# A recurrent attention and mixer kernel: own-step products from PSUM, a new order of work, two units turned by DMA, deeper buffers

## The chip, the cores and the metric

The kernel runs on one core of a Trainium2 chip. A core has five engines with a queue of instructions each: TensorE (PE) multiplies matrices out of SBUF into PSUM, VectorE (DVE) and ScalarE (ACT) work element by element on both memories, GpSimd (POOL) does so on SBUF alone, and SyncE (SP) issues DMA transfers. POOL issues transfers too. The metric is the device time of one execution in microseconds; smaller is better.

## The reference

Four batches, eight heads, 768 steps, 48 columns per head. A state of 48 x 48 per head decays by w in each step and takes in the outer product of k and v. The output of a step reads the state before it, and the step's own product with a weight u in place of the state. The result goes through a mixer: two matrices over the steps (768 to 256 to 768), then two over the columns (384 to 1536 to 384), each pair with a ReLU between and a residual sum.

```python
for t in range(S):
    cur = einsum('bhd,bhe->bhde', u * k[t], v[t])
    y[t] = einsum('bhd,bhde->bhe', r[t], state + cur)
    state = w * state + einsum('bhd,bhe->bhde', k[t], v[t])
h = maximum(xt @ w_tok1, 0) @ w_tok2
u = x + h^T
out = u + maximum(u @ w_ch1, 0) @ w_ch2
```

## The kernel before

A unit is 128 steps of one batch with all eight heads; a batch has six units, numbered 0 to 23 through the batches. Three units make a group, after which the state is carried on (`G = 3`).

The order of all work is written out by hand as a string, `PLAN`. Each word is a step: a letter for the kind, and a unit or indices. The steps are traced in this order, and every engine keeps the order in which its own instructions were traced, so a step that waits holds up all that its engine has behind it. A capital letter is the same step on another engine, mostly DVE. The letters:

- `l0`, `l1`, `l2`: the next load of k, r or v, 192 KB, issued on SP. The n-th load of each belongs to unit n. The list `FIRST` issues k0, k1, r0 and k2 ahead of the plan. `AFTER` makes the load of k with a given number wait until a part of the weights has landed; since SP works in order, all later loads wait behind it. There are seven buffers for each of k, r and v.
- `D`: one of six tables of decay (`wkr`), written by ACT. `C`: small constants.
- `k`, `r` (POOL) or `K`, `R` (DVE): k or r of a unit times its decay, into a tile `kr` with both. `NK` such tiles are used in turn.
- `a`: PE turns the eight blocks of `kr` into one PSUM bank (`kr_ps`, k's half and r's half), and ACT copies the whole to `krT`. `q`: the same with the copy split, k's half by ACT and r's half by DVE. `A`: a DMA transpose issued by SP in place of both.
- `o`: own product, `krT`'s k half times its r half on DVE. `e` / `E`: four small matmuls of it on PE and a copy to `adg` by ACT / DVE. `y` / `Y`: `yd` = v times `adg`, on POOL / DVE.
- `v` / `V`: v as bfloat16 (`vb`) by ACT / DVE. `b`: the scores (`at_ps`) on PE, masked by DVE into `AT`. `s` / `S`: the unit's k and v into the state sum (`kv_ps`) on PE, copied by ACT / DVE (twice 48 partitions), or, for the last unit of a group, scaled by DVE. `c`: the unit's output `y_ps` on PE, plus `yd` on DVE into `x_b`.
- `h`, `g`: the mixer over the steps; `n` / `N` / `t`: the turned `uT` by PE with a copy by ACT / DVE, or by a DMA transpose. `u` / `U`: 128 of the 1536 hidden columns, three matmuls into `z_ps` and a ReLU into `zr` by ACT / DVE. `d`: six matmuls into `h_ps` (h2), after the second half a sum by DVE and a store issued by SP.
- `W`: a part of the weights, issued by POOL in its own order, numbered 0 to 6: 0 and 1 the step matrices, 2 to 4 the up matrix in pieces of 3, 3 and 6 blocks, 5 and 6 the halves of the down matrix.
- `x`: one dummy matmul that keeps PE busy.

PSUM has one bank or two for the scores, the state sum and the output, with one buffer of each (`psA`), and a pool of four banks for all the rest, the dummy matmuls too (`psM`, tag `m`). A bank is free again when all its readers are done.

Engine instructions carry the line of a helper (L68) in the profile, so groups go by tile names.

Of the kernel before, what the change touches and what calls it, by code (L numbers as in the profile page):

```python
# [22 lines left out]
def kernel(  # L23
# [373 lines left out]
    PLAN = """
    l1 D0.0 l1 D0.1 K1 K0 D1.0 l2 D0.2 D1.2 R0 K2 l0 D1.1 x r1 a0 v0 C0 l2 o0 r2 C1 a1 l1 r3 b0
    K3 l1 l0 a2 x e0 x y0 l2 o1 l2 o2 s0 x x x x x x x e1 a3 C2 v1 e2 b1 l0 r4 c0 l1 l2 x x x x
    x x b2 l2 x v2 y1 S1 k4 o3 K5 q4 x x x x x e3 y2 W0 c1 o4 v3 b3 r5 l2 a5 o5 l1 c2 s2 l0 l0  # L400
    W1 x W2 x l1 v5 x x e4 l2 y4 b4 y3 c3 e5 V4 s3 h0.0 b5 y5 W4 x x x s4 c4 h0.1 x c5 h0.2 h0.3
    h0.4 W3 h0.5 g0.1 g0.0 g0.2 l1 g0.5 n0.1 N0.2 N0.0 g0.4 N0.5 k6 l0 l2 g0.3 U0.0.2 u0.0.0
    n0.3 l0 U0.0.7 n0.4 r6 l2 U0.0.8 q6 l1 u0.1.7 u0.0.11 K7 u0.0.6 v6 u0.1.9 o6 r7 U0.0.1
    u0.1.0 W5 R8 l0 u0.0.3 q7 l1 u0.0.9 u0.1.3 u0.0.10 l2 K8 l1 u0.0.5 U0.1.11 u0.1.2 u0.1.6 V7
    e6 U0.1.5 a8 b6 o7 S6 u0.1.4 Y6 U0.0.4 l0 o8 u0.1.1 u0.1.10 e7 W6 y7 l2 b7 d0.1.0 r10 s7 K9
    d0.0.0 k10 l0 c6 E8 b8 R9 l1 u0.1.8 v10 l2 l1 d0.0.1 V9 l1 l0 l2 c7 R11 d0.1.1 a9 l0 d0.2.0
    o9 y8 v8 d0.3.0 S8 c8 b9 a10 e9 l1 K11 d0.2.1 s9 y9 c9 b10 o10 a11 d0.3.1 d0.4.0 k12 o11 r13
    e10 r12 d0.4.1 l0 Y10 c10 v11 v12 l2 l0 e11 b11 s10 Y11 h1.0 d0.5.0 l1 l1 a12 h1.1 c11 v13
    o12 h1.2 h1.3 k13 l0 h1.4 R14 l2 h1.5 l0 d0.5.1 r15 l0 l0 l2 E12 l2 g1.2 g1.0 g1.1 l1 g1.4
    n1.0 k14 n1.2 b12 n1.1 n1.4 g1.5 a13 g1.3 u1.0.0 u1.0.7 o13 l1 Y12 U1.0.1 n1.3 E13 Y13 k15  # L410
    s12 l1 u1.0.4 b13 n1.5 a14 u1.0.5 c12 a15 l2 k16 u1.0.6 o14 U1.0.2 l0 o15 u1.0.3 c13 s13
    u1.0.10 R17 E14 l2 e15 b14 r16 u1.0.8 a16 k17 v14 U1.1.2 l1 u1.0.11 Y14 V15 l0 b15 d1.0.0
    S14 u1.0.9 a17 l2 b16 c14 k18 v16 V17 Y15 d1.1.0 d1.0.1 o16 c15 d1.1.1 U1.1.5 s15 o17 b17
    e16 r19 U1.1.1 r18 y16 l0 c16 E17 l2 v18 s16 l1 u1.1.0 l1 y17 u1.1.3 a18 V20 u1.1.4 o18 k19
    u1.1.6 u1.1.7 c17 h2.0 A19 R20 k21 v19 d1.2.0 E18 b18 l2 k20 R21 h2.1 Y18 h2.2 d1.2.1 h2.3
    o19 h2.4 h2.5 s18 b19 a20 c18 E19 u1.1.8 u1.1.10 o20 v21 r22 l2 g2.0 t2.0 y19 g2.2 c19 g2.5
    e20 a21 g2.1 g2.4 k22 y20 s19 b20 t2.2 o21 u1.1.9 t2.4 r23 n2.1 U1.1.11 g2.3 V23 k23 s20 A22
    c20 u2.0.0 V22 t2.3 b21 E21 u2.0.2 d1.3.0 u2.0.8 d1.3.1 U2.0.6 U2.0.4 b22 o22 n2.5 Y21
    u2.0.1 u2.0.5 U2.0.3 d1.4.0 d1.5.0 u2.1.3 A23 b23 e22 o23 d1.4.1 S21 d1.5.1 e23 u2.0.11 c21
    u2.1.5 Y22 u2.0.7 U2.0.10 Y23 u2.0.9 d2.0.0 c22 u2.1.2 S22 h3.0 h3.1 d2.0.1 c23 h3.2 d2.1.0  # L420
    h3.3 h3.4 u2.1.9 h3.5 d2.1.1 g3.0 g3.1 t3.1 g3.2 d2.2.0 t3.2 t3.0 d2.2.1 u2.1.1 u2.1.7
    u2.1.6 u2.1.4 u2.1.10 g3.3 t3.3 g3.4 U2.1.8 U2.1.0 g3.5 u3.0.1 u3.0.10 U3.0.5 U3.0.6 U2.1.11
    d2.4.0 u3.0.8 t3.4 u3.0.2 t3.5 d2.3.0 d2.4.1 U3.1.1 U3.1.4 U3.1.7 d2.3.1 u3.1.8 U3.0.9
    u3.0.11 U3.1.5 u3.0.3 u3.1.6 U3.0.4 u3.1.0 u3.1.2 U3.1.3 d2.5.0 U3.0.0 d2.5.1 u3.1.11 u3.0.7
    d3.0.0 u3.1.9 u3.1.10 d3.0.1 d3.2.0 d3.2.1 d3.1.0 d3.1.1 d3.5.0 d3.5.1 d3.3.0 d3.4.0 d3.3.1
    d3.4.1
    """
# [31 lines left out]
```

## Time and profile before

| | us |
|---|---|
| median of 3 runs | 174.02 (173.68 to 175.73) |
| the profiled execution, its own time | 173.81 |
| its span | 172.1 |
| granted clock of PE | full throughout |
| ACT busy in the span | 78.6 |
| POOL busy in the span | 50.5 |
| DMA queue of SP | 20.65 MB, 57.8% of the 16 engines' span |
| DMA queue of POOL | 3.15 MB, 11.8% |

The profile shows one execution. A group's row has the line, the engine, the operation, out<-in with tile names, shapes and the number of instructions; behind the bar stand the busy time, the mean of one in ns, and the idle time of the engine before them with what ended it. A timeline's row has the start, the time to the end of the last of the merged instructions, and in brackets the idle time before it. A row of a DMA issue ends with the time from issue to landing. Matmuls overlap, so the duration of a merged matmul row holds more than its share of the engine: eight transposes take 0.45 us when others follow. Weight loads of PE (PEld) run beside matmuls.

### The profile page before, as it was taken

How to read it: one execution, taken by the hardware profiler on the slowest of the kernel's cores; microseconds unless marked ns; L12 is line 12 of the kernel's file. 1: busy time of each engine (PE TensorE's matmuls, PEld its weight loads, DVE VectorE, ACT ScalarE, POOL GpSimd, SP SyncE). 2: the span in 40 equal slices, each digit the busy share in tenths (PEclk: the TensorE clock that was granted, in tenths of full speed). 3: DMA queues.
4: the chain of work that ended last, by engine and by line, in shares of the span. 5: the costliest groups of instructions: out<-in, count | busy, mean ns of one | idle time of the engine just before them, and what ended most of it. 6: DMA issues, size and time to landing. Idle time of an engine off the chain costs nothing.

```text
span 172.1 us, 3977 instructions
## 1 busy us (share of the span) xinstructions
PE 163.1 (95%) x1570; PEld 103.8 (60%) x1570; DVE 121.6 (71%) x231; ACT 78.6 (46%) x172; POOL 50.5 (29%) x61
## 2 busy tenths in 40 slices
PE   6999789899999999999999999899999999999992
PEld 3555565566666766567667677556665655656560
DVE  5476996974797999999997899885655272631312
ACT  3895342179635355399627476331412522334000
POOL 2159946260017392533244919000000000000000
PEclk9999999999999999999999999999999999999999
DMA  5999899999989998999968962540211241201222
GB/s 111 225 221 223 133 196 209 199 150 173 200 176 179 216 236 235 216 230 195 217 141 188 126 140 50 107 107 6 91 41 50 57 107 23 91 0 50 91 91 91
DMA packets 89532, 24.05 MB, mean 140 GB/s; under 512 B 82729, under 2 KB 89514, under 8 KB 89514
## 3 DMA queue, kind: packets, MB, share of 16 engines
q1 hardware_dynamic: 85664, 20.65, 57.8%
q0 software_dynamic: 3824, 3.15, 11.8%
q8 instruction: 12, 0.20, 0.5%
q14 instruction: 6, 0.05, 0.1%
q10 hardware_dynamic: 26, 0.00, 0.0%
HBM read 20.45 MB, written 4.72 MB: 146 GB/s over the span
## 4 chain that ended last, share of the span: by engine, by line
PE 68%; DVE 13%; DMA 6%; issue 5%; ACT 3%; POOL 2%; SPq 1%; POOLq 0%
PE z_ps L68 24%; PE h_ps L68 23%; PE kr_ps L68 4%; PE idle_ps L68 3%; DMA uT<-u_sb 3%; PE y_ps L68 3%; PE at_ps L68 3%; DVE AT L68 2%; DVE x_b L68 2%; PE hT_ps L68 2%; DMA rt<-in_r_dram 2%; DVE own L68 2%; ACT wkr L68 2%; PE kv_ps L68 2%; PE t_ps L68 2%
## 5 line engine op out<-in xcount | busy, mean ns | idle before, releaser
L68 PE MATMUL z_ps<-uT,wch 128*128 128x384 bf16 x288 | 53.6, 326 | 0.8 <-DMA uT<-u_sb 0.8
L68 PE MATMUL h_ps<-wch,zr 128*128 128x384 bf16 x288 | 52.2, 326 | 0.1
L68 ACT ACTIVATE zr<-z_ps 128x384 bf16<-128x384 f32 x66 | 31.7, 494 | 37.6 <-PE z_ps L68 37.4
L68 PEld LDWEIGHTS <-zr 128*128 128x128 bf16 x288 | 27.2, 98 | 17.6 <-DVE zr L68 0.5
L68 PEld LDWEIGHTS <-wch 128*128 128x128 bf16 x288 | 26.6, 98 | 16.7 <-DMA uT<-u_sb 0.6
L68 DVE TENSOR_TENSOR AT<-at_ps,mask 128x1024 bf16<-128x1024 f32 x24 | 29.2, 1215 | 4.1 <-PE at_ps L68 4.1
L68 DVE TENSOR_TENSOR osb<-u_sb,h_ps 128x384 f32<-128x384 bf16 x24 | 13.2, 550 | 18.2 <-PE h_ps L68 18.2
L68 ACT COPY krT<-kr_ps 128x1024 bf16<-128x1024 bf16 (+1 forms) x21 | 20.0, 952 | 8.4 <-PE kr_ps L68 7.8
L68 POOL TENSOR_TENSOR kr<-rt,wkr 128x384 bf16<-128x384 f32 x16 | 17.0, 1071 | 18.5 <-DMA rt<-in_r_dram 9.3
L68 DVE TENSOR_SCALAR zr<-z_ps 128x384 bf16<-128x384 f32 x30 | 16.2, 554 | 8.2 <-PE z_ps L68 8.0
L68 POOL TENSOR_TENSOR kr<-kt,wkr 128x384 bf16<-128x384 f32 x15 | 15.9, 1069 | 12.3 <-PE kv_ps L68 7.0
L68 PEld LDWEIGHTS <-kr 128*128 128x128 bf16 x248 | 16.6, 102 | 4.6 <-issue 0.7
L68 POOL TENSOR_TENSOR yd<-vt,adg 128x384 f32<-128x384 f32 x13 | 11.5, 885 | 25.1 <-DVE yd L68 10.5
L68 DVE TENSOR_TENSOR own<-krT 128x512 bf16<-128x512 bf16 x24 | 13.5, 568 | 3.0 <-ACT krT L68 2.9
L68 DVE TENSOR_TENSOR x_b<-y_ps,yd 128x384 bf16<-128x384 f32 x24 | 13.2, 549 | 2.4 <-PE y_ps L68 1.9
L68 PEld LDWEIGHTS <-krT 48*128 48x128 bf16 (+1 forms) x272 | 10.6, 96 | 6.4 <-issue 3.1
L68 PE MATMUL idle_ps<-warm 128*128 128x512 bf16 x38 | 13.1, 465 | 1.4 <-DVE warm L68 1.4
L68 PE MATMUL kr_ps<-ident,kr 128*128 128x128 bf16 x168 | 14.1, 232 | 0.1
L68 DVE TENSOR_TENSOR u_sb<-x_b,hT_ps 128x384 bf16<-128x384 bf16 x24 | 12.1, 544 | 2.6 <-PE hT_ps L68 2.6
L68 PEld LDWEIGHTS <-wtok 128*128 128x128 bf16 x96 | 8.3, 97 | 5.2 <-issue 1.0
L68 ACT CAST S<-kv_ps 48x192 bf16<-48x192 f32 x24 | 7.5, 313 | 7.7 <-PE kv_ps L68 5.8
L68 PE MATMUL hT_ps<-h1r,wtok 128*128 128x384 bf16 x48 | 10.2, 325 | 0.6 <-ACT h1r L68 0.4
(59 smaller groups left out, 141.5 us busy)
## 6 DMA issues: line engine op xcount, KB each, us to landing
kt<-in_k_dram SPq DMA_DIRECT2D x24, 192.0 KB, 3.8
rt<-in_r_dram SPq DMA_DIRECT2D x24, 192.0 KB, 3.8
vt<-in_v_dram SPq DMA_DIRECT2D x24, 192.0 KB, 3.8
out_dram<-osb SPq DMA_DIRECT2D x24, 192.0 KB, 1.9
wch<-in_moe_w_ch_dram POOLq DMA_DIRECT2D x3, 576.0 KB, 8.3
wtok<-in_moe_w_tok_dram POOLq DMA_DIRECT2D x2, 384.0 KB, 7.4
wch<-in_moe_w_ch_dram POOLq DMA_DIRECT2D x2, 288.0 KB, 9.6
uT<-u_sb SPq DMA_TRANSPOSE x10, 2.3
```

The costliest lines, as they stand in the source:

```text
L68: return lambda *args, **kw: tc.keep_in_program_order(f(*args, **kw))
```

## The change

- `AFTER`: the loads of k8 and k9 both wait for part 3 of the weights. Before, k9 alone waited, for part 2.
- `NK` from 4 to 6, and six buffers of `krT` in place of four.
- A new step `O`: own product with k's half read from `kr_ps` in PSUM and r's half from `krT` in SBUF. It is used for units 0, 1, 2, 3, 4, 6, 11, 12 and 15. The bank `kr_ps` is held until it has run.
- Units 20 and 21 are turned by a DMA transpose (`A`), not by PE and ACT.
- The order is new up to there, with some steps on another engine, among them: k0 on POOL and r1 on DVE; v1 by DVE, v4 by ACT; the copies of adg for units 1 and 3 by DVE; yd of 2 and 4 by DVE; the state copies of unit 1 by ACT; unit 5 with the split copy; r7 by DVE. 24 dummy matmuls stand in the plan in place of 30. From the mixer of batch two on, the order is as before.

```diff
-    AFTER = {9: 2}
+    AFTER = {9: 3, 8: 3}
...
-    NK = 4
+    NK = 6
...
     def turned(n, halves=False):
         L = live[n]
-        krT = apool.tile([128, 2, HP, T], bf16, name="krT")
+        krT = apool.tile([128, 2, HP, T], bf16, name="krT", bufs=6)
         L["kT"], L["rT"] = krT[:, 0], krT[:, 1]
-        kr_ps = psM.tile([128, 2, HP, T], bf16, name="kr_ps", tag="m")
+        kr_ps = L["kr_ps"] = psM.tile([128, 2, HP, T], bf16, name="kr_ps", tag="m")
...
     def turned_by_dma(n):
         L = live[n]
-        krT = apool.tile([128, 2, HP, T], bf16, name="krT")
+        krT = apool.tile([128, 2, HP, T], bf16, name="krT", bufs=6)
...
-    def own_product(n):
+    def own_product(n, from_psum=False):
         L = live[n]
         L["own"] = apool.tile([128, HP, T], bf16, name="own")
-        dve.tensor_mul(L["own"], L["kT"], L["rT"])
+        dve.tensor_mul(L["own"], L["kr_ps"][:, 0] if from_psum else L["kT"], L["rT"])
...
-        o=own_product, e=own_sum, E=lambda n: own_sum(n, copy), y=own_part, Y=lambda n: own_part(n, dve),
+        o=own_product, O=lambda n: own_product(n, True), e=own_sum, E=lambda n: own_sum(n, copy), y=own_part, Y=lambda n: own_part(n, dve),
...
     PLAN = """
-    l1 D0.0 l1 D0.1 K1 K0 D1.0 l2 D0.2 D1.2 R0 K2 l0 D1.1 x r1 a0 v0 C0 l2 o0 r2 C1 a1 l1 r3 b0
-    K3 l1 l0 a2 x e0 x y0 l2 o1 l2 o2 s0 x x x x x x x e1 a3 C2 v1 e2 b1 l0 r4 c0 l1 l2 x x x x
-    x x b2 l2 x v2 y1 S1 k4 o3 K5 q4 x x x x x e3 y2 W0 c1 o4 v3 b3 r5 l2 a5 o5 l1 c2 s2 l0 l0
-    W1 x W2 x l1 v5 x x e4 l2 y4 b4 y3 c3 e5 V4 s3 h0.0 b5 y5 W4 x x x s4 c4 h0.1 x c5 h0.2 h0.3
-    h0.4 W3 h0.5 g0.1 g0.0 g0.2 l1 g0.5 n0.1 N0.2 N0.0 g0.4 N0.5 k6 l0 l2 g0.3 U0.0.2 u0.0.0
-    n0.3 l0 U0.0.7 n0.4 r6 l2 U0.0.8 q6 l1 u0.1.7 u0.0.11 K7 u0.0.6 v6 u0.1.9 o6 r7 U0.0.1
-    u0.1.0 W5 R8 l0 u0.0.3 q7 l1 u0.0.9 u0.1.3 u0.0.10 l2 K8 l1 u0.0.5 U0.1.11 u0.1.2 u0.1.6 V7
-    e6 U0.1.5 a8 b6 o7 S6 u0.1.4 Y6 U0.0.4 l0 o8 u0.1.1 u0.1.10 e7 W6 y7 l2 b7 d0.1.0 r10 s7 K9
-    d0.0.0 k10 l0 c6 E8 b8 R9 l1 u0.1.8 v10 l2 l1 d0.0.1 V9 l1 l0 l2 c7 R11 d0.1.1 a9 l0 d0.2.0
...
-    u1.1.6 u1.1.7 c17 h2.0 A19 R20 k21 v19 d1.2.0 E18 b18 l2 k20 R21 h2.1 Y18 h2.2 d1.2.1 h2.3
-    o19 h2.4 h2.5 s18 b19 a20 c18 E19 u1.1.8 u1.1.10 o20 v21 r22 l2 g2.0 t2.0 y19 g2.2 c19 g2.5
-    e20 a21 g2.1 g2.4 k22 y20 s19 b20 t2.2 o21 u1.1.9 t2.4 r23 n2.1 U1.1.11 g2.3 V23 k23 s20 A22
...
+    l1 x l1 D0.0 D1.0 l1 D0.2 x l0 D1.2 x R0 D1.1 x k0 x D0.1 K2 K1 a0 l2 C0 v0 l1 R1 a1 C1 K3 x
+    r2 O0 b0 l2 O1 e0 l2 y0 r3 l0 x a2 s0 x x V1 b1 r4 l2 x x k4 O2 E1 x a3 O3 x e2 l0 C2 x s1 y1
+    l1 l2 l0 x b2 v2 l2 c0 l0 S2 W0 q4 K5 x l1 c1 W1 O4 x Y2 v3 l2 b3 E3 r5 x e4 q5 l2 l1 c2 x y3
+    v4 W2 s3 b4 o5 x x x Y4 c3 x h0.0 v5 x e5 s4 b5 h0.1 W4 c4 h0.2 y5 c5 h0.3 h0.4 l1 h0.5 g0.1
+    g0.0 W3 g0.2 g0.5 n0.1 N0.2 N0.0 g0.4 g0.3 n0.5 k6 U0.0.2 U0.0.7 l0 n0.4 u0.0.8 U0.0.0 r6 l2
+    l1 n0.3 K7 u0.0.11 u0.0.6 q6 u0.1.2 u0.1.7 l2 l0 l1 U0.1.9 W5 R7 v6 O6 l0 U0.0.1 b6 u0.1.3
+    u0.0.3 l2 u0.0.9 R8 U0.1.0 q7 K8 u0.0.5 u0.0.10 U0.1.11 l1 e6 V7 s6 u0.1.6 a8 u0.1.4 l0 s7 o7
+    U0.1.5 l1 U0.1.1 l2 E7 u0.1.10 W6 o8 Y6 U0.0.4 c6 b7 d0.1.0 Y7 e8 l0 d0.0.0 v9 d0.0.1 l1 l0
...
+    e9 l1 K11 d0.2.1 y9 c9 s9 l0 b10 o10 a11 d0.3.1 l2 d0.4.0 E10 R13 v11 k12 O11 d0.4.1 Y10 v12
+    c10 r12 e11 s10 l0 h1.0 b11 Y11 h1.1 l0 d0.5.0 l2 l1 l0 a12 R14 c11 O12 r15 k13 l1 v13 l1
...
+    u1.0.5 l2 l2 k16 a14 c12 a15 l0 o14 u1.0.3 c13 s13 O15 U1.0.10 v14 E14 r17 l1 r16 b14 K17
...
+    l2 s16 l1 d1.0.1 l1 y17 u1.1.3 a18 V20 u1.1.4 R20 k21 o18 k19 u1.1.6 u1.1.7 c17 R21 h2.0 k20
+    A19 v19 d1.2.0 E18 b18 l2 h2.1 Y18 A20 h2.2 d1.2.1 h2.3 o19 h2.4 h2.5 s18 b19 c18 E19 u1.1.8
+    u1.1.10 o20 v21 r22 A21 l2 g2.0 t2.0 y19 g2.2 c19 g2.5 e20 g2.1 g2.4 k22 y20 s19 b20 t2.2 o21
...
```

More of the change, by code (lines that the diff above doesn't have):

```diff
@@ L404 @@
-    u0.1.0 W5 R8 l0 u0.0.3 q7 l1 u0.0.9 u0.1.3 u0.0.10 l2 K8 l1 u0.0.5 U0.1.11 u0.1.2 u0.1.6 V7
-    e6 U0.1.5 a8 b6 o7 S6 u0.1.4 Y6 U0.0.4 l0 o8 u0.1.1 u0.1.10 e7 W6 y7 l2 b7 d0.1.0 r10 s7 K9
-    d0.0.0 k10 l0 c6 E8 b8 R9 l1 u0.1.8 v10 l2 l1 d0.0.1 V9 l1 l0 l2 c7 R11 d0.1.1 a9 l0 d0.2.0
-    o9 y8 v8 d0.3.0 S8 c8 b9 a10 e9 l1 K11 d0.2.1 s9 y9 c9 b10 o10 a11 d0.3.1 d0.4.0 k12 o11 r13
-    e10 r12 d0.4.1 l0 Y10 c10 v11 v12 l2 l0 e11 b11 s10 Y11 h1.0 d0.5.0 l1 l1 a12 h1.1 c11 v13
-    o12 h1.2 h1.3 k13 l0 h1.4 R14 l2 h1.5 l0 d0.5.1 r15 l0 l0 l2 E12 l2 g1.2 g1.0 g1.1 l1 g1.4
@@ L410 @@
[L410 to L414, printed above, removed]
-    u1.1.6 u1.1.7 c17 h2.0 A19 R20 k21 v19 d1.2.0 E18 b18 l2 k20 R21 h2.1 Y18 h2.2 d1.2.1 h2.3
@@ L416 @@
-    o19 h2.4 h2.5 s18 b19 a20 c18 E19 u1.1.8 u1.1.10 o20 v21 r22 l2 g2.0 t2.0 y19 g2.2 c19 g2.5
-    e20 a21 g2.1 g2.4 k22 y20 s19 b20 t2.2 o21 u1.1.9 t2.4 r23 n2.1 U1.1.11 g2.3 V23 k23 s20 A22
[L418 to L426, printed above, removed]
+    l1 x l1 D0.0 D1.0 l1 D0.2 x l0 D1.2 x R0 D1.1 x k0 x D0.1 K2 K1 a0 l2 C0 v0 l1 R1 a1 C1 K3 x
+    r2 O0 b0 l2 O1 e0 l2 y0 r3 l0 x a2 s0 x x V1 b1 r4 l2 x x k4 O2 E1 x a3 O3 x e2 l0 C2 x s1 y1
@@ new lines @@
+    R10 u0.1.8 k10 R9 l2 v8 l2 d0.3.0 b8 d0.1.1 l1 v10 k9 l0 c7 R11 S8 a9 d0.2.0 o9 y8 c8 b9 a10
+    e9 l1 K11 d0.2.1 y9 c9 s9 l0 b10 o10 a11 d0.3.1 l2 d0.4.0 E10 R13 v11 k12 O11 d0.4.1 Y10 v12
+    c10 r12 e11 s10 l0 h1.0 b11 Y11 h1.1 l0 d0.5.0 l2 l1 l0 a12 R14 c11 O12 r15 k13 l1 v13 l1
+    h1.2 h1.3 h1.4 h1.5 d0.5.1 g1.2 g1.0 g1.1 l2 n1.2 l0 g1.4 n1.0 b12 l1 g1.3 l2 e12 n1.1 K14
+    a13 k15 n1.4 l0 U1.0.1 y12 u1.0.7 u1.0.0 o13 N1.3 g1.5 u1.0.2 E13 Y13 l1 u1.0.4 s12 b13 N1.5
+    u1.0.5 l2 l2 k16 a14 c12 a15 l0 o14 u1.0.3 c13 s13 O15 U1.0.10 v14 E14 r17 l1 r16 b14 K17
@@ new lines @@
+    u1.0.8 U1.0.11 u1.1.2 y14 e15 a16 V15 b15 l0 l2 d1.0.0 V17 U1.0.6 u1.0.9 S14 b16 a17 V16 k18
+    d1.1.0 Y15 c14 o16 U1.1.5 d1.1.1 c15 o17 s15 e16 u1.1.1 y16 l0 r18 b17 u1.1.0 r19 c16 e17 V18
+    l2 s16 l1 d1.0.1 l1 y17 u1.1.3 a18 V20 u1.1.4 R20 k21 o18 k19 u1.1.6 u1.1.7 c17 R21 h2.0 k20
+    A19 v19 d1.2.0 E18 b18 l2 h2.1 Y18 A20 h2.2 d1.2.1 h2.3 o19 h2.4 h2.5 s18 b19 c18 E19 u1.1.8
+    u1.1.10 o20 v21 r22 A21 l2 g2.0 t2.0 y19 g2.2 c19 g2.5 e20 g2.1 g2.4 k22 y20 s19 b20 t2.2 o21
+    u1.1.9 t2.4 r23 n2.1 U1.1.11 g2.3 V23 k23 s20 A22 c20 u2.0.0 V22 t2.3 b21 E21 u2.0.2 d1.3.0
@@ new lines @@
+    u2.0.8 d1.3.1 U2.0.6 U2.0.4 b22 o22 n2.5 Y21 u2.0.1 u2.0.5 U2.0.3 d1.4.0 d1.5.0 u2.1.3 A23
+    b23 e22 o23 d1.4.1 S21 d1.5.1 e23 u2.0.11 c21 u2.1.5 Y22 u2.0.7 U2.0.10 Y23 u2.0.9 d2.0.0 c22
+    u2.1.2 S22 h3.0 h3.1 d2.0.1 c23 h3.2 d2.1.0 h3.3 h3.4 u2.1.9 h3.5 d2.1.1 g3.0 g3.1 t3.1 g3.2
+    d2.2.0 t3.2 t3.0 d2.2.1 u2.1.1 u2.1.7 u2.1.6 u2.1.4 u2.1.10 g3.3 t3.3 g3.4 U2.1.8 U2.1.0 g3.5
+    u3.0.1 u3.0.10 U3.0.5 U3.0.6 U2.1.11 d2.4.0 u3.0.8 t3.4 u3.0.2 t3.5 d2.3.0 d2.4.1 U3.1.1
+    U3.1.4 U3.1.7 d2.3.1 u3.1.8 U3.0.9 u3.0.11 U3.1.5 u3.0.3 u3.1.6 U3.0.4 u3.1.0 u3.1.2 U3.1.3
@@ L427 @@
+    d2.5.0 U3.0.0 d2.5.1 u3.1.11 u3.0.7 d3.0.0 u3.1.9 u3.1.10 d3.0.1 d3.2.0 d3.2.1 d3.1.0 d3.1.1
+    d3.5.0 d3.5.1 d3.3.0 d3.4.0 d3.3.1 d3.4.1
     """
```

## The prediction

> **What bounds the kernel now.** I read the page first, then the windows of the stages, the groups by form, and the timelines of DVE, POOL and SP up to 50 us.
>
> ```profile
> span 172.1 us, 3977 instructions
> PE 163.1 (95%) x1570; PEld 103.8 (60%) x1570; DVE 121.6 (71%) x231; ACT 78.6 (46%) x172; POOL 50.5 (29%) x61
> ...
> 9.00:29.50 20.50, 18.54 (x237) 11.74 (x237) 17.52 (x27) 10.69 (x28) 13.93 (x17) 1.00 1.17 194
> ...
> 33.60:47.00 13.40, 13.40 (x115) 8.64 (x113) 8.83 (x19) 10.00 (x21) 2.65 (x3) 1.00 1.13 173
> 47.00:70.00 23.00, 22.68 (x274) 15.40 (x272) 21.17 (x37) 10.50 (x23) 11.62 (x11) 1.00 0.96 209
> 70.00:97.00 27.00, 26.83 (x332) 18.53 (x332) 24.94 (x46) 18.75 (x41) 11.64 (x13) 1.00 0.92 193
> 97.00:108.00 11.00, 10.62 (x138) 7.40 (x135) 10.74 (x21) 5.76 (x13) 6.37 (x7) 1.00 0.59 93
> ...
> 33.63 0.65 PE L68 MATMUL z_ps<-uT,wch 128*128 128x384 bf16 x3
> ```
>
> The window rows give the stretch, then busy time of PE, PEld, DVE, ACT and POOL, granted clock, DMA share and GB/s. From 33.6 us, where the first up-projection starts, PE works without gaps (13.40 of 13.40, 22.68 of 23, 26.83 of 27). Before that PE is filled with dummy matmuls, and DVE is the busiest of the others, 17.52 of 20.50 us. From 97 to 108 us DVE is full (10.74 of 11). So three things can move the end: when the first z starts; PE work after it; and stalls of PE in between. The window 33.6 to 97 holds only 0.5 us of PE idle, so almost nothing is to be gained there and much can be lost.
>
> **The start, to 33.6 us.** Units 0 to 5 pass through DVE in order.
>
> ```profile
> 9.00:29.50 20.50, 4.70 (x6) 1.00 1.17 194
> ...
> L68 DVE TENSOR_TENSOR own<-krT x24: 406/417/1236, 9.4 to 119.3; 128x512 bf16<-128x512 bf16 x24
> ...
> 11.93 1.00 POOL L68 TENSOR_TENSOR kr<-rt,wkr 128x384 bf16<-128x384 f32 x1 [2.12 <-DMA rt<-in_r_dram]
> 12.88 1.01 POOL L68 TENSOR_TENSOR yd<-vt,adg 128x384 f32<-128x384 f32 x1
> ...
> 11.96 2.20 DVE L68 TENSOR_TENSOR own<-krT 128x512 bf16<-128x512 bf16 x2
> 15.28 1.22 DVE L68 TENSOR_TENSOR AT<-at_ps,mask 128x1024 bf16<-128x1024 f32 x1 [1.11 <-PE at_ps L68]
> ...
> 17.32 1.22 DVE L68 TENSOR_TENSOR AT<-at_ps,mask 128x1024 bf16<-128x1024 f32 x1 [0.36 <-PE at_ps L68]
> ...
> 28.72 0.56 DVE L68 TENSOR_TENSOR x_b<-y_ps,yd 128x384 bf16<-128x384 f32 x1 [0.71 <-PE y_ps L68]
> ```
>
> The first row is DVE's own products alone: six take 4.70 us, where six of the median 417 ns take 2.50. The other 2.20 us are stretch: two own products from 11.96 to 14.16 us ran while POOL was at kr and yd (11.93 to 13.89). The masks (AT) and x_b, which read one operand from PSUM, keep 1.22 and 0.56 us beside POOL work, so own products with k's half in PSUM should lose the stretch. Their own duration isn't in the trace:
>
> ```profile
> L68 DVE TENSOR_TENSOR AT<-at_ps,mask 128x1024 bf16<-128x1024 f32 x24 | 29.2, 1215 | 4.1 <-PE at_ps L68 4.1
> ...
> L68 DVE TENSOR_TENSOR x_b<-y_ps,yd 128x384 bf16<-128x384 f32 x24 | 13.2, 549 | 2.4 <-PE y_ps L68 1.9 <-POOL yd L68 0.3
> ...
> L68 DVE TENSOR_TENSOR yd<-vt,adg 128x384 f32<-128x384 f32 x11 | 6.8, 614 | 0.1
> ...
> L68 DVE COPY adg<-ad_ps 128x8 f32<-128x8 f32 x8 | 1.2, 153 | 0.1
> ...
> L68 DVE COPY krT<-kr_ps 128x512 bf16<-128x512 bf16 x3 | 1.3, 424 | 1.6 <-ACT krT L68 1.5
> ...
> L68 DVE CAST S<-kv_ps 48x192 bf16<-48x192 f32 x8 | 2.8, 352 | 0.2
> ```
>
> Between 549 ns for 384 columns and 1215 for 1024, 512 columns stand at 0.68 us; the lower bound is the 0.417 of today. I take 0.68, since those two rows also mix PSUM and SBUF. The Trainium skill (VectorE: DVE Perf Modes, the perf-mode tier table) speaks against the edit: a two-tensor operation drops from twofold to single rate as soon as an operand lies in PSUM. By its cycle formula for a PSUM source, (120 + 512) at 0.96 GHz, the estimate would be 0.66 us, so the sum would come out 0.1 us lower; no run shown here has this operation.
>
> DVE's list for units 0 to 5 then changes by: stretch -2.20; S1 leaves for its matching step on ACT, two casts of 0.352, -0.70; five O products at +0.26, +1.32; yd of units 2 and 4 come from POOL, +1.23; adg of units 1 and 3 come from ACT, +0.31; r's half of unit 5 comes from ACT, +0.42. Casting v and writing kr keep their counts. Net +0.38 us of work.
>
> What the order can win is idle time: 20.50 - 17.52 = 2.98 us. The waits of 1.11 and 0.36 us came because unit 1's score matmuls stood on PE behind e1, a3 and e2, which needed o1 and o2; now b1 stands ahead of O2. I take these 1.47 us as gone. The 0.71 before the last x_b stays: y_ps has one buffer. Against that, K3 now stands ahead of O0 and b0 on DVE and blocks them until k3 has landed.
>
> ```profile
> 5.33 0.97 SPq L68 DMA_DIRECT2D vt<-in_v_dram  x1
> 6.34 0.70 SPq L68 DMA_DIRECT2D kt<-in_k_dram  x1
> 7.09 0.79 SPq L68 DMA_DIRECT2D vt<-in_v_dram  x1
> ...
> kt<-in_k_dram SPq DMA_DIRECT2D x5, 192.0 KB, 3.7
> ...
> 9.45 0.63 DVE L68 TENSOR_TENSOR own<-krT 128x512 bf16<-128x512 bf16 x1 [1.71 <-ACT krT L68]
> ...
> 41.50 0.55 DVE L68 TENSOR_TENSOR kr<-kt,wkr 128x384 bf16<-128x384 f32 x1
> ```
>
> k3 is the eighth load before and after, so it lands near 6.34 + 3.7 = 10.0; with a kr product of 0.55 us (the last row) O0 starts near 10.55 instead of 9.45. K3's own 0.55 isn't lost, so +0.55. v0 moves from the seventh load to the ninth, from 5.33 to near 7.09 on SP, and ACT's copy of a1 stands behind v0; O1 needs that copy, but it stands behind O0 and AT0 on DVE, which cover it. Two more buffers of kr cost two more memsets, in DVE's idle time before wkr is there. The six dummy matmuls less cost nothing: they fill gaps. Start: -1.47 + 0.38 + 0.55 = -0.5 us, with bounds -2.6 (no idle left) and +1.5 (new order with no gain, two POOL collisions of DVE's new yd as long as the ones lost). POOL's queue: W2 moves behind y3, so its issue is some 3 us later, but the weights leave that queue one after another and the one ahead is still under way; free unless W2 lands after 33 us.
>
> **Units 6 to 19.** New places and engines: three more ReLUs, two more kr and the yd of unit 7 come to DVE, a cast, a state copy and a uT copy leave it. DVE has 4.6 us free from 33.6 to 47 and 1.8 from 47 to 70, so I put zero, bounds -0.3 and +1.5. O6, O11, O12 and O15 hold a PSUM bank until DVE has multiplied, about a microsecond longer; with three other banks, zero.
>
> **Units 20 and 21.**
>
> ```profile
> 40.06 0.45 PE kr_ps L68 x8
> ...
> L68 ACT COPY krT<-kr_ps 128x1024 bf16<-128x1024 bf16 x18 | 18.2, 1013 | 7.2 <-PE kr_ps L68 6.6 <-ACT adg L68 0.5
> ...
> krT<-kr SPq DMA_TRANSPOSE x3, 4.3
> ...
> 94.40 3.41 POOL L68 TENSOR_TENSOR kr<-kt,wkr 128x384 bf16<-128x384 f32 x3
> ...
> 102.51 0.41 DVE L68 TENSOR_TENSOR own<-krT 128x512 bf16<-128x512 bf16 x1
> ...
> 104.69 3.35 DMA uT<-u_sb
> ```
>
> PE loses twice 0.45 = 0.9 us and ACT two copies of 1.0. But PE waits next for a uT that lands at 108.04 and that DVE, full there, set off. So the bounds are -0.9 and 0 if nothing is late; I take half, -0.4. Late would be: k20 is ready on POOL at 97.81, SP can issue A20 there, 4.3 us bring 102.1, and o20 ran at 102.51. Cover of 0.4 us; behind it on SP wait the load of v22 or v23 and one store, both early.
>
> **Sum.** -0.5 - 0.4 = -0.9 us. The profiled execution took 173.81 (172.1 span and 1.7 around it), 0.2 under the median of 174.02. From the median: 173.1.
>
> **The rivals.** First, the wait on weights. k8 used to be free and k9 waited for W2; now both wait until W3 has landed, with every later load behind them on SP.
>
> ```profile
> 30.56 5.58 SPq L68 DMA_DIRECT2D kt<-in_k_dram  x1
> ...
> 37.41 0.61 SPq L68 DMA_DIRECT2D kt<-in_k_dram  x1
> ...
> 26.14 1.57 POOL L68 DMA_DIRECT2D wch<-in_moe_w_ch_dram  x2
> ...
> wch<-in_moe_w_ch_dram POOLq DMA_DIRECT2D x1, 288.0 KB, 10.0
> ...
> kt<-in_k_dram SPq DMA_DIRECT2D x1, 192.0 KB, 11.3
> ...
> 44.34 0.61 PE L68 MATMUL kr_ps<-ident,kr 128*128 128x128 bf16 x8
> ```
>
> W3 is the second of the POOL issues at 26.14, near 26.9, and landed 10.0 us later, at 36.9. A k8 issued then lands between 40.6 (3.7 us, a free queue) and 48.2 (11.3 us, as k9 did from 37.41 beside the last weights). K8 on DVE ran at 41.50 and PE turned unit 8 at 44.34. From a landing at about 43.5 PE stalls; at the late end 48.2 + 0.55 - 44.3 = 4.4 us. For it: W5 and W6 no longer wait on POOL for r7, so they stand behind W3 at once. Against: with SP held, the loads' queue runs empty and k8 is its first. It gives 173.1 to 177.5, in the middle 175.3. Chance 0.25.
>
> Second, the start doesn't fill: DVE's idle stays and the added work counts. -0.9 turns to 1.47 - 0.9 = +0.6, and collisions of Y2 and Y4 with POOL, up to a microsecond as at 11.96, bring 174.5 to 175.5. That is also the case in which O does nothing: with one ACT copy for both halves, O still waits for that copy because it reads r's half from it. Chance 0.18.
>
> The Trainium skill (SBUF — State Buffer, Who interferes with whom) lets a DVE operation with at most one SBUF input, outside the two-port modes, run free of GpSimd. By that rule O can't be stretched, and Y2 and Y4, with two SBUF inputs, can.
>
> Third, better: DVE runs through (-2.6) and all 0.9 us of PE count: 170.5 to 172. Chance 0.15.
>
> **The numbers.** The forecast case, 173.1 with its own range of 172 to 174.5, has 0.42. The range 171.0 to 176.3 leaves out the late end of the first rival (0.12) and the best of the third (0.07). Two per cent, about what a measurement of this kernel can tell from no change, is 3.5 us. Faster by that needs the third rival's far end: 0.06. Slower by that, above 177.5, needs the first rival's late end with a start that wins nothing, or a jam of banks: 0.13. Within: 0.81.
>
> **What would show it.** In the changed profile: own products near 0.68 us and none near 1.1 in the start; AT of unit 1 near 14 us in place of 15.28; the first z near 33 us; no PE gap before the transposes of unit 8, and kr of unit 8 on DVE with no DMA wait; between 97 and 108 us no own product that waits for a DMA transpose. A first z later than 33.6, or a DMA wait of k8 of over a microsecond, makes the forecast wrong.

## The result and the profile after

| | before | after |
|---|---|---|
| median, us | 174.87 (173.68 to 175.73, 4 runs) | 180.56 (180.47 to 181.48, 4 runs) |
| the profiled execution, its own time | 173.81 | 180.65 |
| its span | 172.1 | 178.9 |

The ratio is 1.034, with a 95% interval of 1.028 to 1.040: slower, and above the range of the prediction. Ratios here and below leave out runs more than 1.5% above the fastest run of the same kernel. In the page of the kernel after, the span, the row of PE and the row of the granted clock (40 slices of 4.5 us):

```profile
span 178.9 us, 3914 instructions
...
PE 163.4 (91%) x1548; PEld 102.1 (57%) x1548; DVE 124.8 (70%) x240; ACT 76.0 (42%) x168; POOL 46.3 (26%) x57
...
PEclk9999999998589999999999999999999999999999
```

PE's busy time is 163.4 us, as before (163.1), while the span grew by 6.8. Either PE stood still or its matmuls took longer; the clock row points to slices 10 to 12, some 40 to 54 us. The windows of the stages that the prediction showed, now of the kernel after:

```profile
9.00:29.50 20.50, 16.22 (x240) 10.60 (x239) 15.97 (x30) 11.14 (x28) 13.08 (x16) 1.00 1.11 196
33.60:47.00 13.40, 9.29 (x70) 5.40 (x68) 6.73 (x13) 6.19 (x13) 0.00 (x0) 0.88 1.14 185
47.00:70.00 23.00, 23.00 (x244) 15.33 (x243) 18.40 (x35) 11.56 (x25) 6.17 (x7) 0.92 0.86 178
70.00:97.00 27.00, 26.00 (x314) 17.62 (x312) 25.81 (x46) 15.35 (x31) 8.97 (x9) 1.00 0.83 172
```

From 33.6 to 47 us PE is busy for 9.29 us, where it was 13.40 of 13.40, and the clock falls to 0.88. This is the stage in which the prediction saw "almost nothing is to be gained there and much can be lost" and then wrote zero. Timeline of PE after, around the hole:

```profile
39.72 1.15 PE L68 MATMUL z_ps<-uT,wch 128*128 128x384 bf16 x6
44.97 2.10 PE L68 MATMUL z_ps<-uT,wch 128*128 128x384 bf16 x6 [4.11 <-DVE own L68]
46.87 1.06 PE L68 MATMUL kr_ps<-ident,kr 128*128 128x128 bf16 x8
47.72 3.02 PE L68 MATMUL z_ps<-uT,wch 128*128 128x384 bf16 x9
50.58 0.24 PE L68 MATMUL ad_ps<-wu_blk,own 128*128 128x2 bf16 x4
```

PE stands for 4.11 us until DVE has done an own product. Behind that, six z matmuls take 2.10 us in place of 1.15, and eight transposes 1.06 in place of 0.61 at 36.90: the windows of 44 to 46, 46 to 48 and 48 to 50 us have a granted clock of 0.50. By the starts of successive groups against those of groups of the same size at full rate, the stretch from 39.7 to 51 us loses 4.27 us to the stand and 0.92 + 0.40 + 1.39 = 2.7 to the slow matmuls, together 7.0. That is the whole 6.8 of the span; all other edits come to about zero in sum. What the stand waits for is in the chain of waits of the kernel after (start, length, what; "issue" is a wait for nothing that is shown):

```profile
26.60 17.40 DMA rt<-in_r_dram
44.00 0.02 issue
44.02 0.56 DVE kr L68
44.58 0.34 DVE own L68
44.93 0.05 issue
44.97 2.10 PE z_ps L68 x6
```

The load of r7 took 17.4 us from issue to landing. R7, which the change moved to DVE, stands at the head of DVE's queue until then, and behind it O6. The z matmuls wait for the PSUM bank that O6 still has to read. Why the load is late is in the timelines of POOL. First before, then after:

```profile
30.38 0.99 POOL L68 TENSOR_TENSOR kr<-rt,wkr 128x384 bf16<-128x384 f32 x1
35.02 1.00 POOL L68 TENSOR_TENSOR kr<-rt,wkr 128x384 bf16<-128x384 f32 x1 [3.65 <-DMA rt<-in_r_dram]
35.96 1.71 POOL L68 DMA_DIRECT2D wch<-in_moe_w_ch_dram  x2
```

```profile
29.37 1.00 POOL L68 TENSOR_TENSOR kr<-rt,wkr 128x384 bf16<-128x384 f32 x1
30.31 1.70 POOL L68 DMA_DIRECT2D wch<-in_moe_w_ch_dram  x2
```

Before, r7 on POOL waited 3.65 us for its load, and the issues of W5 and W6 (576 KB each) stood behind it, until 35.96. This was a brake: the weights let the loads go first. With r7 on DVE nothing of POOL stands ahead of them, and they leave at 30.31, 5.65 us earlier, into the queue beside r7's load. The DMA view of 27 to 37 us (packets, MB, share of the 16 engines; q0 is POOL's queue, q1 is SP's), before and then after:

```profile
q0 software_dynamic: 1139, 1.13, 67.2%
q1 hardware_dynamic: 4097, 0.77, 44.7%
```

```profile
q0 software_dynamic: 1664, 1.54, 93.4%
q1 hardware_dynamic: 2219, 0.42, 28.6%
...
rt<-in_r_dram SPq DMA_DIRECT2D x2, 192.0 KB, 17.4
```

The loads get 0.42 MB in these 10 us in place of 0.77. By the counts a packet of the weights has 1.54 MB / 1664 = 925 bytes, one of the loads 189. The Trainium skill (DMA: Bandwidth & Descriptors, Queues, rings and completion order) says that each DMA engine takes turns between its queues by the packet. These numbers fit that roughly: the queue of the small packets moved 2219 of them beside 1664, not far from one for one, and about a quarter of the bytes. Whether a packet that the profile counts is a packet in the page's sense, no run here shows.

One more part of the delay is the new order of the loads: r7's is the 24th, behind v7, where it was the 23rd, ahead of v7. SP's rows of its issue, and the time to landing, before (the landing by the DMA view of that moment) and then after:

```profile
21.73 3.66 SPq L68 DMA_DIRECT2D rt<-in_r_dram  x1
rt<-in_r_dram SPq DMA_DIRECT2D x1, 192.0 KB, 13.2
```

```profile
26.60 9.84 SPq L68 DMA_DIRECT2D rt<-in_r_dram  x2
```

So r7 lands 9.1 us later, 4.9 of it because it is issued later and 4.2 because it is longer under way.

### The profile page after: what moved, and what is told of

It is laid out like the page before. It is cut to its first block, busy times and chain, and to the rows that moved or that the text cites. A ratio compares the mean times of both kernels' runs of the same rounds, so it can differ in the third digit from the quotient of the medians.

```text
span 178.9 us, 3914 instructions
## 1 busy us (share of the span) xinstructions
PE 163.4 (91%) x1548; PEld 102.1 (57%) x1548; DVE 124.8 (70%) x240; ACT 76.0 (42%) x168; POOL 46.3 (26%) x57
## 4 chain that ended last, share of the span: by engine, by line
PE 53%; SPq 14%; DMA 13%; DVE 10%; issue 6%; ACT 1%; POOL 1%; POOLq 0%; DVEq 0%; ACTq 0%
PE h_ps L68 23%; PE z_ps L68 21%; SPq L68 14%; DMA rt<-in_r_dram 10%; DVE AT L68 3%; DVE u_sb L68 3%; PE y_ps L68 2%; PE at_ps L68 2%; PE kr_ps L68 2%; DMA kt<-in_k_dram 2%; DMA vt<-in_v_dram 2%; PE hT_ps L68 1%; DVE x_b L68 1%; PE kv_ps L68 1%; DVE yd L68 1%
## 5 line engine op out<-in xcount | busy, mean ns | idle before, releaser
L68 PE MATMUL z_ps<-uT,wch 128*128 128x384 bf16 x288 | 56.9, 336 | 4.1 <-DVE own L68 4.1
L68 ACT ACTIVATE zr<-z_ps 128x384 bf16<-128x384 f32 x63 | 30.6, 491 | 43.7 <-PE z_ps L68 43.5
L68 DVE TENSOR_SCALAR zr<-z_ps 128x384 bf16<-128x384 f32 x33 | 17.6, 553 | 8.3 <-PE z_ps L68 8.2
L68 ACT COPY krT<-kr_ps 128x1024 bf16<-128x1024 bf16 (+1 forms) x19 | 17.4, 922 | 11.7 <-PE kr_ps L68 11.7
L68 POOL TENSOR_TENSOR yd<-vt,adg 128x384 f32<-128x384 f32 x12 | 10.2, 850 | 40.9 <-ACT adg L68 27.2
L68 PEld LDWEIGHTS <-kr 128*128 128x128 bf16 x232 | 15.1, 101 | 4.8 <-issue 2.1
L68 POOL TENSOR_TENSOR kr<-rt,wkr 128x384 bf16<-128x384 f32 x13 | 14.0, 1088 | 3.3 <-DMA rt<-in_r_dram 2.4
L68 PE MATMUL kr_ps<-ident,kr 128*128 128x128 bf16 x152 | 12.2, 227 | 0.0
L68 DVE TENSOR_TENSOR kr<-rt,wkr 128x384 bf16<-128x384 f32 x11 | 7.3, 675 | 6.7 <-DMA rt<-in_r_dram 4.5
L68 ACT CAST S<-kv_ps 48x192 bf16<-48x192 f32 x28 | 8.7, 312 | 4.6 <-PE ad_ps L68 2.6
```

The lines of the kernel that those rows point to most:

```text
L68: return lambda *args, **kw: tc.keep_in_program_order(f(*args, **kw))
```

## The experiments

Each kernel ran beside the kernel before on the same chip; ratios are to that, below 1 is faster.

**r7 back on POOL, ahead of W5.** From the kernel after:

```diff
- U0.1.9 W5 R7 v6 O6
+ U0.1.9 r7 W5 v6 O6
```

> The changed kernel with r7 multiplied on POOL ahead of W5, as before the change, in place of on DVE behind W5. Theory of POOL's queue (the 2.4 MB of W5 and W6 left 5.6 us earlier because POOL no longer waits for r7, and starve the loads): r7 lands near 37 in place of 44.0, no PE gap of 4.1 us after 40.9, clock stays at 1.00, 173 to 174.5 us. Theory of the gate (k8 and k9 behind W3): nothing changes, about 180.

174.1 us, ratio 1.001 (0.996 to 1.006). POOL's timeline of this kernel has the brake again:

```profile
36.64 1.00 POOL L68 TENSOR_TENSOR kr<-rt,wkr 128x384 bf16<-128x384 f32 x1 [6.17 <-DMA rt<-in_r_dram]
37.58 1.71 POOL L68 DMA_DIRECT2D wch<-in_moe_w_ch_dram  x2
```

PE is busy 9.90 of 10 us from 40 to 50 at full clock. One step moved back returns the whole loss. r7's load is issued at 26.60 here too, but takes 10.0 us in place of 17.4: with the weights held back, the later issue leaves no stand. (W5 and W6 are 1.18 MB, two of 576 KB; the 2.4 MB of the expectation is what POOL's queue moved in all while r7 was under way in the kernel after, 2.36 MB from 26.6 to 44 us.)

**The gate alone.** `AFTER` as before, all else as after:

```diff
- AFTER = {9: 3, 8: 3}
+ AFTER = {9: 2}
```

> The changed kernel with the gate of before: k9 alone waits, for part 2. Theory of the gate: the loads behind k8 come early again, 173 to 175.5 us. Theory of POOL's queue: r7 is issued ahead of k8, so it still lands near 44 and PE still stands still from 41 to 45: 179 to 182.

179.17 us, ratio 1.023 (1.013 to 1.033). R7 still waits 4.26 us on DVE and PE stands 3.90. The gate of k8 and k9 isn't the cause; the two ratios, 1.034 and 1.023, have intervals that overlap, so up to some 1% may still be its part.

**The move alone, in the kernel before.**

```diff
- o6 r7 U0.0.1
+ o6 R7 U0.0.1
```

> The kernel before with one letter changed: r7 times its decay on DVE in place of POOL, so that W5 and W6 leave POOL behind r6. Theory of POOL's queue: they are issued near 31.5 in place of 36, r7 lands 2 to 6 us later than its 34.9, DVE waits for it at about 38.5 and the units behind it follow: 175.5 to 179. Theory of the gate or of the new order: as before the change, 174 to 175.

176.74 us (174.77 to 180.05, 10 runs), ratio 1.008 (1.003 to 1.013). Its profile is of the slowest of these runs, so it shows a stand but not what the ratio measures. DVE's timeline, and then PE's:

```profile
38.24 0.55 DVE L68 TENSOR_TENSOR kr<-rt,wkr 128x384 bf16<-128x384 f32 x1
...
45.82 0.56 DVE L68 TENSOR_TENSOR kr<-rt,wkr 128x384 bf16<-128x384 f32 x1 [6.34 <-DMA rt<-in_r_dram]
```

```profile
46.77 3.04 PE L68 MATMUL z_ps<-uT,wch 128*128 128x384 bf16 x9 [4.51 <-DVE krT L68]
```

R7 is the first row and waits for nothing; the late load is that of r8, issued at 32.72 where it was 29.55. PE stands behind it as in the kernel after, and the clock falls to 0.50 (46 to 50 us). k6 and r6 still hold POOL ahead of W5 in the order of before, in this run until 34.22, so that the weights left only 1.7 us earlier than before. So the move costs less in the old order, and the runs spread over 5 us; what makes the difference between them, one kept profile can't show.

**r7 on POOL, between W5 and W6.**

```diff
- U0.1.9 W5 R7 v6 O6
+ U0.1.9 W5 r7 v6 O6
```

> The changed kernel with r7 on POOL, but behind W5 (W6 behind both). It separates the two parts of the POOL theory: if DVE's blocked queue is what costs, DVE runs on and 174 to 176 come out; if the late landing is what costs, PE waits at the transposes of unit 7 instead: W5 alone delays r7 to 39 to 42, 175 to 178. By the theory of the gate about 180.

173.92 us, ratio 0.993 (0.988 to 0.998): a little faster than before. W5 alone left at 29.95 and r7 ran on POOL at 41.17, so r7 is still late, but nothing of DVE's is behind it and W6 waits until 42.12; PE is busy 10.00 of 10 us from 40 to 50.

**r7 on POOL behind both.** W6 moved up, so that DMA is loaded as after, and only DVE is free of r7; PE, ACT and SP keep their order.

```diff
- U0.1.9 W5 R7 v6 O6
+ U0.1.9 W5 W6 r7 v6 O6
```

> The changed kernel with r7 on POOL behind both W5 and W6, so that DVE isn't held but the weights leave as early as in the changed kernel. If the blocked queue of DVE is the cost, 173.5 to 175; if the late landing is (r7 near 44, unit 7's transposes on PE behind it), PE stands still from about 42 to 45 all the same: 177 to 180.

Four runs: 175.23, 178.51, 179.43 and 179.55 us, beside 175.44 for the kernel before, so three show most of the loss and one none; there is no ratio. The timelines of POOL and of PE in the slowest:

```profile
44.01 0.99 POOL L68 TENSOR_TENSOR kr<-rt,wkr 128x384 bf16<-128x384 f32 x1 [11.90 <-DMA rt<-in_r_dram]
```

```profile
45.05 0.61 PE L68 MATMUL kr_ps<-ident,kr 128*128 128x128 bf16 x4 [2.91 <-POOL kr L68]
```

With DVE free, PE goes on until unit 7's own transposes and stands there for 2.91 us, and the clock falls to 0.53 (46 to 48 us). So in this run the late load alone makes PE stand, with DVE free; in the kernel after, with DVE held, PE stands 1.2 us longer. How the loss divides between the late load and the held DVE, four runs so far apart don't settle. Against the run before, only W6 has moved: with it held back until 42.12, r7 ran at 41.17 and PE never stood.

**r7 loaded earlier.** The load of r7 is moved ahead of those of v6 and v7, from the 24th to the 22nd.

```diff
- Y2 v3 l2 b3 E3 r5 x e4 q5 l2 l1 c2
+ Y2 v3 l1 b3 E3 r5 x e4 q5 l2 l2 c2
```

> The changed kernel with r7 loaded ahead of v6 and v7 (22nd load in place of 24th), R7 still on DVE and W5 and W6 still early. If the loads' queue starves behind the weights, place in that queue decides: r7 lands at 33 to 38, DVE's wait of 4.5 us goes, v7 lands late in its place (near 44) and costs 0 to 2 us at its cast on DVE: 174 to 177. If the landing depends on when W5 and W6 end and not on the place, 179 to 181.

176.91 us (175.3 to 178.13), ratio 1.011 (1.005 to 1.016). R7 ran at 39.64 without a wait; then R8 waited on DVE, and PE behind it:

```profile
44.47 0.56 DVE L68 TENSOR_TENSOR kr<-rt,wkr 128x384 bf16<-128x384 f32 x1 [2.36 <-DMA rt<-in_r_dram]
```

```profile
45.55 0.65 PE L68 MATMUL z_ps<-uT,wch 128*128 128x384 bf16 x3 [2.13 <-DVE zr L68]
```

An earlier place moves the stand to the next load and halves it. The clock stayed at 1.00 through this shorter stand.

**Dummy matmuls in the stand, 18 and then 8.** They are to keep PE busy while it stands; they go to the output's bank, which is idle then. The kernel after with `keep_warm_y(18)`, and with 8 in its place:

```diff
+ for _ in range(n):
+     z_ps = psA.tile([128, 512], f32, name="idle_y", tag="y")
+     pe.matmul(z_ps, warm[:, 0:128], warm, start=True, stop=True)
...
- u0.0.3 l2 u0.0.9 R8
+ u0.0.3 X l2 u0.0.9 R8
```

> The changed kernel with 18 dummy matmuls (18 x 0.215 = 3.9 us) in the idle bank of the output, traced where PE stands still from 40.9 to 45.0; r7 still comes late. If the idle PE costs its clock (1.00 before the gap, 0.50 from 44 to 50), the clock stays near 1.00 and the 2.7 us lost behind the gap return: 177 to 178.5 us. If the matmuls behind the gap are slow because their results are fetched slowly, or the clock falls anyway, 180 to 181.

With 18: 182.68 us, ratio 1.043 (1.038 to 1.049). In its profile the stand that they were to fill isn't there. POOL's rows:

```profile
33.61 1.00 POOL L68 TENSOR_TENSOR kr<-rt,wkr 128x384 bf16<-128x384 f32 x1 [2.78 <-DMA rt<-in_r_dram]
34.55 1.71 POOL L68 DMA_DIRECT2D wch<-in_moe_w_ch_dram  x2
```

Here r6 landed late, and its wait on POOL held W5 and W6 back until 34.55, 4.2 us later than in the kernel after. The load of r7 then took 8.2 us, and R7 ran at 40.02 without a wait: here r6's wait was the brake that r7's is in the kernel before. So the dummy matmuls only delay PE, by 0.43 us each, 7.72 in all, where the expectation had 0.215. The clock stayed at 1.00, and six z behind them took 1.14 us; what the clock is worth couldn't be read from this run.

> The changed kernel with 8 dummy matmuls in the output's idle bank ahead of the first matmul that stood still at 40.9 us. Eighteen of them took 7.72 us, 0.43 us each, so eight take 3.4 of the 4.1 us of the gap and delay nothing. If the halved clock behind the gap costs what the matmul groups there show over full rate (0.92 + 0.40 + 1.39 = 2.7 us), the time falls from 180.6 to near 177.9 us, 1.018 to 1.022 of the kernel before, with a granted clock of 0.9 or more from 44 to 52 us. Rival: the slow matmuls only fill waits that would be there anyway (for r8 and k8 to land), and the time stays within 0.8 us of the changed kernel's, 1.03 or more, though the clock stays up.

With 8: 177.26 us (176.75 to 178.75), ratio 1.019 (1.011 to 1.027). PE's timeline (seven of the eight have a record):

```profile
41.28 2.97 PE L68 MATMUL idle_y<-warm 128*128 128x512 bf16 x7 [0.27 <-PE z_ps L68]
44.08 1.14 PE L68 MATMUL z_ps<-uT,wch 128*128 128x384 bf16 x6
...
47.72 0.61 PE L68 MATMUL kr_ps<-ident,kr 128*128 128x128 bf16 x8
```

From the first z behind the stand to unit 8's transposes it is 47.72 - 44.08 = 3.64 us, where the kernel after needs 51.34 - 44.97 = 6.37: the clock's part is 2.73 us, and the time falls by 3.3 (r7 also landed 1.4 us earlier in this run, which let z start 0.9 earlier). So about 2.7 of the 6.8 us is the clock behind the stand and the rest is the stand.

**Parts of the change.** The next four start from the kernel with r7 between W5 and W6 (ratio 0.993), to see what each other edit is worth. Own products from SBUF (`O` does what `o` does):

> The kernel of the fourth run (r7 on POOL behind W5) with all own products read from SBUF again. If the products from PSUM pay by escaping POOL's lock, the six of the start stretch from 2.5 to 3.5 us or more and the time rises by 0.5 to 2 us over that run's ratio of 0.993, to 0.996 to 1.005. If the start is ended by something else, 0.990 to 0.996.

174.07 us, 1.001 (0.997 to 1.005). The six own products of the start take 3.34 us in place of 2.50. The profile kept is of the second slowest of twelve runs, and in it the stretch reaches PE and its clock. DVE's row, PE's, and the window of 20 to 22 us:

```profile
16.00 1.03 DVE L68 TENSOR_TENSOR own<-krT 128x512 bf16<-128x512 bf16 x1
```

```profile
17.09 0.25 PE L68 MATMUL ad_ps<-wu_blk,own 128*128 128x2 bf16 x4 [1.48 <-DVE own L68]
```

```profile
20.00:22.00 2.00, 1.78 (x19) 1.32 (x18) 1.22 (x4) 1.00 (x2) 0.81 (x1) 0.50 0.89 126
```

The granted clock is 0.50 here and 0.75 from 22 to 24 us, and the first z starts at 34.98, not 33.87. So what this run loses isn't the length of the products alone; how much of it the clock has isn't measured.

Units 20 and 21 turned by PE again (`a20`, `a21` at their places of before):

> The kernel of the fourth run with units 20 and 21 turned by PE and ACT again. If PE's 0.9 us count, the ratio rises by 0.005 over 0.993; if DVE ends that stage, it doesn't move (0.990 to 0.996).

175.22 us, 1.008 (1.005 to 1.012). In its timeline PE has a wait that neither the kernel after nor the next two have:

```profile
110.07 0.65 PE L68 MATMUL z_ps<-uT,wch 128*128 128x384 bf16 x3 [1.32 <-DMA uT<-u_sb]
```

The buffers of before (`NK = 4`, four of `krT`):

> The kernel of the fourth run with four buffers of kr and krT. kr of unit 10 and on then waits for a state step four units back. With PE covered as before the change, the ratio stays near 0.993 (to 1.0); if the new order needs the room, 1.005 to 1.02.

172.97 us, 0.9955 (0.991 to 1.000). The gate of before:

> The kernel of the fourth run with the gate of before (k9 alone waits, for part 2). If the gate to part 3 costs by holding k8 and all loads behind it, 0.980 to 0.990; if it helps by keeping loads away from the weights, 0.996 to 1.005; if neither, 0.993.

173.2 us, 0.996 (0.993 to 1.000). No worth of the buffers or the gate can be seen here. Both back at once:

> The changed kernel with r7 on POOL between W5 and W6, the gate of before (k9 alone, part 2) and the buffers of before. The gate and the buffers were each worth nothing when taken back alone (0.996 and 0.9955 beside 0.993), so theory: 0.990 to 0.997, the whole gain comes from order, O and the two DMA transposes. Rival: gate and buffers each cover for the other, and without both the time is over 1.00.

172.25 us (171.9 to 172.59), 0.989 (0.981 to 0.997). So the gain needs neither: the order, `O` and the two DMA transposes are enough, and this is, with the next one, the fastest that was found.

**Own products from PSUM in the kernel before.** Units 0 to 4 use `O`, nothing else is changed:

> The kernel before with the own products of units 0 to 4 read from PSUM and nothing else. By the lock between DVE and POOL the six own products of the start take 2.5 us in place of 4.7 and the first up-projection starts 0.5 to 2 us before 33.6: 172.5 to 174. If what ends the start is something else (the output's single bank, the last units' chain), no change: 174 to 175.

174.13 us beside 175.44 for the kernel before in the same runs, ratio 0.989 (0.984 to 0.994). The own products of the start fall from 4.70 us to 2.41. The profile, of the slowest of six runs, doesn't show where the gain comes from: DVE's wait for the scores of unit 1 grows from 1.11 to 2.62 us, AT of unit 1 is at 15.61, and the first z starts at 33.82, no earlier than the 33.63 of before. With units 20 and 21 by DMA on top:

> The kernel before with two parts of the change alone: O for units 0 to 4, and units 20 and 21 turned by DMA. If both gains stand by themselves and add (0.989 for the first, about 0.99 for the second), near 0.98, 171 us. If the units 20 and 21 gain only in the new order, or the start's gain was spread between runs, 0.985 to 0.995.

173.37 us, 0.996 (0.991 to 1.000). The two gains don't add, in the order of before; the intervals of the two runs overlap, so whether the second edit gives back part of the first or the first was measured a little too well is open. All ratios of these parts lie within 2% of 1, and the medians of the kernel before beside them go from 174.17 to 175.44, so they rank the parts only as far as the intervals lie apart.

## Why the prediction was wrong

**Units 6 to 19 (the step that failed).** The prediction put "zero, bounds -0.3 and +1.5" here and worked it out from DVE's free time: two more kr "come to DVE". It counted R7 as work that fits into this. Its price wasn't work, but two waits. One is on the engine it left: W5 and W6 are in POOL's queue behind r7, and without r7's wait they go 5.65 us earlier, against the very load that R7 needs. The other is on the engine it came to: R7 holds DVE until that load has landed. The order of the loads adds to it, issuing r7's 4.9 us later; the prediction didn't price that. Both waits were to be read before: POOL's row at 35.02 has the wait for the load in its brackets, and the issue of the weights is the next row. Putting r7 back on POOL ahead of W5 gave 1.001. With r7 on POOL behind both weights, three of four runs kept most of the loss, so the late load can make it without DVE; how it divides between the two waits stays open. The prediction gave 0.13 to a time above 177.5, for the late end of its first rival or "a jam of banks"; neither was worked out for r7.

**The first rival.** It said "W5 and W6 no longer wait on POOL for r7, so they stand behind W3 at once", and used this only as a point for a late k8. The sentence was right and named the cause; the load that it made late was r7, issued before the gate, not k8. Its place (unit 8's transposes), its price (4.4 us) and its mechanism (the gate) don't stand: K8 ran at 48.92 with no DMA wait, and with the gate taken back the loss stayed. That the stand is near the 4.4 us is a coincidence.

**No clock in the sum.** The prediction let a stand cost its own length. Here 4.1 us cost 6.8, as the matmuls behind it ran at half rate.

**Banks held by O6.** Priced at zero "with three other banks". While O6 ran when due, that holds; when R7 held O6 up, the bank of unit 6 was the one that z waited for. The stand doesn't need it: with the move alone in the kernel before, where no bank is held by an own product, PE stood for 4.51 us in the kept run, behind DVE's copy of unit 7.

**The start.** Forecast -0.5, with the first z near 33. It started at 33.63 in both kernels. Two terms were wrong and go against each other. First, `O` costs no more than `o`: by form, in the kernel after,

```profile
L68 DVE TENSOR_TENSOR own<-krT x15: 407/424/1180, 25.1 to 126.2; 128x512 bf16<-128x512 bf16 x15
L68 DVE TENSOR_TENSOR own<-kr_ps,krT x9: 409/416/424, 11.9 to 87.9; 128x512 bf16<-128x512 bf16 x9
```

416 ns in place of the 0.68 us taken, so the term of +1.32 us is +0, and no `O` is stretched (424 ns is its longest, where `o` has 1180). The lower bound was the right end. The rule of the Trainium skill that was weighed there (VectorE: DVE Perf Modes, the perf-mode tier table, single rate for a two-tensor operation with any PSUM operand, 0.66 us by its formula) doesn't hold for this operation: the measurement decides. O of unit 1 at 13.36 and of unit 2 at 15.42 took 0.41 us each beside POOL's work (12.89 to 16.76). That POOL doesn't stretch them agrees with the Trainium skill (SBUF — State Buffer, Who interferes with whom).

Second, "the six dummy matmuls less cost nothing: they fill gaps". There are fewer, but five of them now stand ahead of unit 0's transposes in PE's queue. PE's timeline of the kernel after, and DVE's:

```profile
6.90 2.31 PE L68 MATMUL idle_ps<-warm 128*128 128x512 bf16 x5
9.01 1.34 PE L68 MATMUL kr_ps<-ident,kr 128*128 128x128 bf16 x16
```

```profile
11.05 0.34 DVE L68 TENSOR_TENSOR wu_blk<-wud 64x4 bf16<-64x4 f32 x2 [2.23 <-ACT wud L68]
11.41 0.56 DVE L68 TENSOR_TENSOR kr<-kt,wkr 128x384 bf16<-128x384 f32 x1
11.89 0.42 DVE L68 TENSOR_TENSOR own<-kr_ps,krT 128x512 bf16<-128x512 bf16 x1
...
14.28 1.22 DVE L68 TENSOR_TENSOR AT<-at_ps,mask 128x1024 bf16<-128x1024 f32 x1 [0.24 <-PE at_ps L68]
...
28.83 0.56 DVE L68 TENSOR_TENSOR x_b<-y_ps,yd 128x384 bf16<-128x384 f32 x1 [0.71 <-PE y_ps L68]
```

Unit 0 is turned at 9.01 where it was 7.31, and O0 runs at 11.89, not near 10.55. K3's wait for k3 was not what held it: DVE waits 2.23 us for `wud`, which ACT writes behind its copy of unit 0, now at 9.94 in place of 8.40. The waits ahead of the masks went as forecast (AT of unit 1 at 14.28, "near 14"), and DVE's work fell to 15.97 us from 17.52; but its last x_b is at 28.83, where it was 28.72. DVE's idle time in this window rose as much as its work fell, from 2.98 to 4.53 us: of the 1.47 us forecast as gone 0.24 stays, and a new wait stands ahead of O0. The start of the first z differs by up to a microsecond between profiles of nearly the same order (33.24 with the gate taken back, 34.17 with the 18 dummy matmuls, which stand behind it), so 0.5 us can't be judged from one of them.

**Units 20 and 21.** Right in sign, too small: -0.4 forecast, bounds -0.9 and 0. Undone, they cost 1.008 against 0.993 to 0.996, or 1.2 to 1.5%, 2.1 to 2.7 us. The bound counted PE's 0.9 us and took the wait for uT, which DVE sets off, as staying. The wait went as well: 1.32 us when PE turns the units, none with the two DMA transposes. Against the run with gate and buffers back, the run with PE's turns is 1.8 us behind on DVE's work throughout this stage, and its PE, 2.0 behind just ahead of the wait (unit's output at 108.39 and 106.38), is 3.5 behind after it (z at 110.07 and 106.60). So 1.5 us are lost there. DVE sets the three transposes of u off at the same distance, but SP's issue of them takes 4.64 us in place of 3.79, which is 0.85 of it. Why, no run here shows; the rest of the 2.1 to 2.7 us isn't placed either. No own product waits more than 0.2 us for a DMA transpose, as forecast.

**W2 behind y3, buffers, gate.** Free, as priced, so far as the intervals show; no matmul of the kernel after waits for W2.

## What to carry to other kernels

Before a step is moved off an engine that also issues transfers, read the row behind it in that engine's queue: if the step waits for data, its wait is a brake on the transfers behind it, and without it they run into the loads that the others need. A step that waits for a load belongs on an engine whose next instructions can wait as long, and the load's landing time has to be taken again under the new traffic, not from the old trace. A stand of PE is to be priced with the slow matmuls behind it: here every stand of 2.91 us and more was followed by half the clock.
